# Packed output projections in four groups of 160 columns, and the fold's turn on VectorE

## The chip, the core and the metric

The kernel runs on one core of one Trainium2 chip. The metric is the device time of one execution in microseconds (us). Three executions of the kernel before took 4691.0, 4698.19 and 4706.44 us; the median is 4698.19 us. One further execution was taken with the hardware profiler; every row of a profile shown here is of that one.

A core has TensorE (PE in the rows; PEld are its weight loads), VectorE (DVE), ScalarE (ACT), GpSimd (POOL) and SyncE (SP). Each takes its own instructions in their written order and waits on semaphores for the others. SP only issues DMAs here; POOL issues DMAs too, and so, rarely, does ACT.

## The reference, cut to what matters

The program computes a forward pass and all gradients of two blocks that share a normalised input. Block B is a gated MLP over 2048 tokens of width 640. Block A, the one that matters here, is attention with a recurrent memory: the 2048 tokens are cut into T = 64 segments of 32, and each segment sees 8 memory rows that come from the output of the segment before.

```python
for s in range(n_seg):
    h = jnp.concatenate([mem, xs], axis=1)      # 8 memory rows and 32 tokens
    q, k, v = h @ Wq, h @ Wk, h @ Wv            # 32 heads of width 128
    p = softmax(where(mask, q @ k.T * scale, -1e9))
    o = einsum('bhte,hed->btd', p @ v, Wo)      # output projection: a sum over 32 heads of 128
    mem = o[:, :M, :]                           # 8 rows of 640 into the next segment
```

The memory makes block A serial: segment t+1 cannot begin before the 8 rows of segment t have been through the output projection. The gradient has the same chain backwards: the gradient of the 8 memory rows of segment t is a sum of three such projections, of the gradients of v, k and q with the weights turned, and segment t-1 needs it.

## The kernel before, in words

The work stands in phases: LayerNorm and the MLP forward; the forward recurrence (`recurrence`, L555); the backward recurrence (`phase4_Abwd`, L1083); the weight gradients; the MLP backward. Within the two recurrences the instruction order of every engine is the written order (`in_order`, L273, chains each engine's instructions). There is no scheduler that moves anything.

**A step.** Each recurrence calls `chain(t, gap)` once per segment, the forward one for t = 0 to 63, the backward one for t = 63 to 0. `chain` holds what depends on the memory rows, and at named places it calls `gap("W0")`, `gap("W1")`, ... `gap("G6")`. A gap puts work that does not depend on this step's memory in between: attention of the 32-token rows of the group of three segments before, in units of four heads (three units in most steps). In the forward recurrence such a unit goes through `scores`, `soft_max`/`soft_exp`, `norm` (a multiplication on POOL), `turn_p` (four transposes on PE and a copy on DVE, L835 to L841) and `pv`. In the backward one it goes through `ld` (four loads, all on SP's queue, L1289 to L1311), `turn`, `dprob`, `dsoft` (on DVE, L1350 and L1353) and `gmem`. A gap may end with `WARM` matmuls (L915, L1430), whose result nobody reads.

**The way round a forward step.** `hx` holds h transposed, 640 as five chunks of 128 partitions, with columns 0 to 7 for memory and 8 to 31 for tokens. `packed_half` (L301) multiplies it with Wk, Wq and Wv: the array of PE is used as four column groups of 32, each with its own 512 columns of weights as the moving operand. Then come the scores of the 8 memory rows, their softmax, P times v (L682), and `oTm` (L684, L685), the result transposed. `packed_out` (L317) is the output projection. Its rows are few, so it too uses four column groups: group 2a+b takes heads 16a to 16a+15 and output columns 320b to 320b+319. A call is 16 rounds of four matmuls with 320 moving columns, and every call leaves four partial results in the bank `pm`: two halves of the heads, times two halves of the columns.

The four parts are then folded and turned. `fold_add` (L330) lets ACT copy partitions 64 to 127 out of the bank (L334) and DVE add them to partitions 0 to 63 (L336, two halves), which gives `fsum` with 64 partitions: 32 rows for each half of the columns. `fold_turn` (L346) transposes the 8 memory rows with six small matmuls on PE against a selection matrix (L352). DVE copies the result into the next step's `hx` (L699), and the next step's Wk matmuls (L306) may start. `fsum` goes to the scratch tensor `FS` by one DMA from POOL (L700), and the gaps G5 and G6 stand around these pieces:

```python
packed_out(k, pm, oTm, Wo, True, True)
fs = fold_add(k, pm, ch)
gap("G5")
pt = fold_turn(k, bC, fs)
nc.vector.tensor_copy(nxt[:, :, 0:8], pt[:])
nc.gpsimd.dma_start(k.FS[t], fs[:])
gap("G6")
```

**The way round a backward step.** The same helpers are used. `packed_half` with WoT gives the gradient of o; the gradients of v (`gvT`), k (`gkT`) and q (`gqT`) of the memory rows follow; three `packed_out` calls with WvT, WkT and WqT accumulate into one bank (the first two cut in two pieces each, 5 + 11 and 4 + 12 rounds, around other work). Then `fold_add`, `gap("G4")`, `fold_turn`, `gap("G5")`, the copy into `gox` (the backward `hx`, L1283), and two DMAs from POOL into `GWO` (`fold_store`, L340 to L343), `gap("G6")`.

**Queues.** In a regular backward step SP issues, in this order: two stores of `dSm` (L1273), a load `xp` (L1174), the four loads of the unit freed in G3, the four of the unit freed in G5, the store of `GOS` (L1215), the four loads of the unit freed in W1, then the loads for the next step (L1151 to L1169). After the recurrences, a list `later` of DRAM-to-DRAM copies from `FS` is issued on POOL, one per backward step.

## Time and profile before

| what | value |
|---|---|
| median of three executions | 4698.19 us |
| the profiled execution | 4684.61 us |
| its span | 4682.7 us, granted clock 0.988 |
| forward recurrence, regular steps 3 to 62 | from 444.9 to 1563.8 us, a step is 18.7 to 19.2 us |
| backward recurrence, 64 steps | from 1821.5 to 2895.0 us, a step is 17.03 us |
| `packed_out` matmuls | 4032 forward, 12288 backward |
| `fold_turn` matmuls | 756 |

The steps were measured from the first matmul of one step's last `packed_out` to that of the next. A row of a view gives a start, a duration, the engine, the line, the operation and the tiles; in the grouped rows a duration is from the start of the first to the end of the last. A matmul's duration is a model, its start is recorded; so rates are read from starts.

### The profile page before, as it was taken

What the parts mean: (1) busy time and instruction counts of PE and PEld (TensorE: products, weight loads), DVE (VectorE), ACT (ScalarE), POOL (GpSimd) and SP (SyncE); (2) the same over time, 40 slices, a digit from 0 to 9 for tenths busy, and PEclk for the clock granted to TensorE, in tenths of its full rate; (3) what the DMA queues carried; (4) which work ended last, traced back from release to release, by engine and by line L of the source; (5) the groups of instructions that cost most, each with busy time, mean ns of one, the idle gap of its engine ahead of it and who ended that gap; (6) DMA issues with size and microseconds to landing.
All of it is one profiled execution on the core that took longest, in us unless ns stands there. A gap on an engine that the chain in (4) does not pass through costs nothing. (4 is left out here: it accounts for less than half of the span.)

```text
span 4682.7 us, 159785 instructions
## 1 busy us (share of the span) xinstructions
PE 4466.5 (95%) x64504; PEld 2821.1 (60%) x64504; DVE 2244.7 (48%) x7156; ACT 1587.4 (34%) x4360; POOL 2098.4 (45%) x3528
## 2 busy tenths in 40 slices
PE   8999999999999898999999998999999999999999
PEld 4544555555555555666666665676667666666675
DVE  8734666666666534555555553343224432311460
ACT  5432555555544433333333332232223322200000
POOL 6532555555555423455444444354335533311440
PEclk9999999999999998999999999999999999999999
DMA  8773566666655677777777775664345543579783
GB/s 269 236 252 119 175 178 178 179 179 179 180 168 167 167 181 230 211 225 207 215 211 209 208 209 154 144 163 132 110 116 158 147 129 107 170 223 207 159 181 100
DMA packets 976843, 834.77 MB, mean 178 GB/s; under 512 B 518890, under 2 KB 858286, under 8 KB 974144
## 3 DMA queue, kind: packets, MB, share of 16 engines
q1 hardware_dynamic: 763879, 547.92, 42.2%
q0 software_dynamic: 129952, 228.13, 16.4%
q10 hardware_dynamic: 82275, 48.52, 4.0%
q8 instruction: 509, 8.34, 0.8%
q14 instruction: 228, 1.87, 0.1%
HBM read 472.66 MB, written 310.33 MB: 167 GB/s over the span
## 5 line engine op out<-in xcount | busy, mean ns | idle before, releaser
L1667 PE MATMUL wg<-gr,hr 128*128 128x512 bf16 x2400 | 521.7, 379 | 0.0
L1648 PE MATMUL g<-land,ghacc 128*128 128x320 bf16 x3072 | 459.9, 300 | 0.8
L1667 PEld LDWEIGHTS <-hr 128*128 128x128 bf16 x2400 | 233.9, 98 | 278.9
L306 PEld LDWEIGHTS <-hx 128*32 128x32 bf16 x10240 | 246.8, 96 | 229.1 <-issue 14.6
L1648 PEld LDWEIGHTS <-ghacc 128*128 128x128 bf16 x3072 | 289.2, 98 | 104.2 <-ACT ghacc L92 2.2
L90 DVE CAST wgo<-wg 128x512 bf16<-128x512 f32 x72 | 49.8, 692 | 471.2 <-PE wg L1667 471.2
L90 DVE CAST stg<-bank 128x512 bf16<-128x512 f32 x256 | 177.1, 692 | 158.6 <-PE bank L306 154.5
L880 POOL DMA_DIRECT2D OR<-xv x163 | 89.8, 551 | 361.1 <-ACT xv L92 338.5
L1613 POOL DMA_DIRECT2D GSP<-grs x48 | 25.5, 542 | 473.1 <-ACT grs L1605 472.0
L92 ACT COPY ghacc<-t6g 128x768 bf16<-128x768 bf16 (+1 forms) x176 | 137.1, 779 | 293.8 <-PE t6g L1630 284.5
L1324 POOL DMA_DIRECT2D VTD<-gvT x176 | 129.4, 742 | 218.7 <-ACT gvT L1323 209.5
L325 PEld LDWEIGHTS <-gkv 128*8 128x8 bf16 x8192 | 177.6, 86 | 82.2 <-issue 4.1
L832 POOL TENSOR_TENSOR xP<-xP,xrz 120x480 bf16<-120x480 bf16 x163 | 161.1, 988 | 76.0 <-DVE xrz L831 46.6
L812 ACT ACTIVATE xP<-xsp,xnm 120x120 bf16<-120x120 f32 (+1 forms) x540 | 186.1, 372 | 26.0 <-DVE xnm L794 25.9
L1654 DVE TENSOR_TENSOR ghacc<-ghacc,g 128x320 f32<-128x320 f32 x192 | 93.6, 487 | 209.9 <-PE g L1648 209.9
L336 DVE TENSOR_TENSOR fsum<-bank,fup 64x160 bf16<-64x160 f32 x254 | 69.5, 311 | 258.5 <-ACT fup L334 255.2
L92 ACT CAST wgo<-wg 128x512 bf16<-128x512 f32 x48 | 28.1, 585 | 479.8 <-PE wg L1667 407.0
L1371 POOL DMA_DIRECT2D GXP<-gks x157 | 91.0, 580 | 189.5 <-ACT gks L1369 188.8
L325 PE MATMUL bank<-Wo,oTm 128*32 128x320 bf16 x4032 | 154.2, 307 | 18.4 <-DVE oTm L684 18.4
L325 PE MATMUL bank<-WkT,gkv 128*8 128x320 bf16 x4096 | 162.8, 299 | 4.2 <-issue 2.2
L325 PE MATMUL bank<-WvT,gkv 128*8 128x320 bf16 x4096 | 166.4, 305 | 0.5 <-DVE gkv L1197 0.5
L306 PE MATMUL bank<-Wq,hx 128*32 128x512 bf16 x2560 | 161.6, 381 | 0.0
(389 smaller groups left out, 10916.1 us busy)
## 6 DMA issues: line engine op xcount, KB each, us to landing
QVS<-stg SPq DMA_DIRECT2D x128, 256.0 KB
kT<-VTD SPq DMA_DIRECT2D x64, 320.0 KB
PR<-xP POOLq DMA_DIRECT2D x168, 120.0 KB, 3.1
VTD<-gvT POOLq DMA_DIRECT2D x168, 120.0 KB, 4.0
land<-DSR SPq DMA_DIRECT2D x168, 120.0 KB
land<-PR SPq DMA_DIRECT2D x168, 120.0 KB
OR<-xv POOLq DMA_DIRECT2D x163, 120.0 KB, 3.0
orr<-OR SPq DMA_DIRECT2D x14, 1280.0 KB
```

The lines of the kernel that those rows point to most:

```text
L90: return nc.vector.tensor_copy(out, in_)
L92: return nc.scalar.copy(out, in_)
L306: k.nc.tensor.matmul(bank[32 * g:32 * g + 32, :], x[:, dc, :], W[:, dc, c0:c0 + 512], start=(dc == 0), stop=(dc == k.DC - 1), tile_positio ...
L325: k.nc.tensor.matmul(pm[p0:p0 + nq, 0:320], x[:, h, :], W[:, h, 320 * b:320 * b + 320], start=(first and i == 0), stop=(last and i == 15), ...
L812: nc.scalar.activation(Pb[0:n, j, 0:n], sp[0:n, j, :], ACT.Exp, bias=nmx[0:n, j:j + 1], scale=k.scale, accum_out=Z[0:n, j:j + 1])
L832: eng.tensor_tensor(Pb[0:n, :, 0:n], Pb[0:n, :, 0:n], bc_last(rz[0:n], n), ALU.mult)
L880: q.dma_start(k.OR[120 * tl:120 * tl + n, c0:c0 + 512], v[0:n])
L1324: nc.gpsimd.dma_start(k.VTD[tl][:, :, h0:h0 + 4, :], vTq[:])
L1371: (nc.sync if (tl, qd) in pro else nc.gpsimd).dma_start(k.GXP[tl, :, qd, 0:ns], ks[:].rearrange("p s i h m -> p s i (h m)"))
L1648: nc.tensor.matmul(pg[:], ring[:, i, j, r0:r0 + P], Ws[qd][i][:, j, 320 * h:320 * h + 320], start=(i == 0 and j == 0), stop=(i == 2 and j ...
L1654: nc.vector.tensor_tensor(a, a, pg[:], ALU.add)
L1667: nc.tensor.matmul(pw[:], hr[:, tl, dc * P:(dc + 1) * P], grs[i][:, tl, :], start=(tl == 0), stop=(tl == NF - 1))
```

## The change

`packed_out` gives each column group 160 output columns over all 32 heads, in place of 320 columns over 16 heads. A call is now 32 rounds of four matmuls with 160 moving columns. Group g takes the columns whose index, in blocks of 32, is g modulo 4: its moving operand is five runs of 32 columns, 128 apart. No partial sums are left, so there is nothing to add. With this choice of columns a transpose of 32x32 blocks puts output column 128c + 32g + r of row m onto partition 32g + r, at place m of block c, which is where `hx` wants it.

`fold` takes the place of `fold_add` and `fold_turn`: one block transpose of the bank on DVE (128x160, fp32), a DVE copy of 8 of every 32 elements into the next `hx`, and then an ACT copy of the bank to bf16 for the store. `fold_store` now has four DMAs, one for each group, with runs of 32 elements (64 bytes), and it is issued on SP in both recurrences, where POOL had one (forward) or two (backward). In the built program these DMAs have the shape 160x1x32 forward and 40x1x32 backward; they stand on SP's queue after the unit loads of G5.

In the gaps: forward, `turn_p` of the second unit moves from G6 to W0 of the next step (after the Wk matmuls), `norm` of the third unit moves up into G5, G6 is gone, and G5's `WARM` goes from two matmuls to one. Backward, the gaps G4 and G5 follow each other after `fold`, and the one `WARM` matmul of G4 is gone. Pieces of the accumulation are cut at the same places (10 + 22 and 8 + 24 rounds). `FS` is now stored in the order of the output, so the `later` list has half as many copies.

```diff
-def packed_out(k, pm, x, W, first, last, i0=0, i1=16):
+def packed_out(k, pm, x, W, first, last, i0=0, i1=32):
 
     nq = x.shape[2]
-    for i in range(i0, i1):
-        for a in range(2):
-            for b in range(2):
-                h = 16 * a + i
-                p0 = 32 * (2 * a + b)
-                k.nc.tensor.matmul(pm[p0:p0 + nq, 0:320], x[:, h, :], W[:, h, 320 * b:320 * b + 320],
-                                   start=(first and i == 0), stop=(last and i == 15),
-                                   tile_position=(0, p0), skip_group_check=True)
+    for h in range(i0, i1):
+        w = W[:, h, :].rearrange("p (c g r) -> p g c r", g=4, r=32)
+        for g in range(4):
+            k.nc.tensor.matmul(pm[32 * g:32 * g + nq, 0:160].rearrange("p (c r) -> p c r", r=32), x[:, h, :], w[:, g],
+                               start=(first and h == 0), stop=(last and h == k.H - 1),
+                               tile_position=(0, 32 * g), skip_group_check=True)
 
-def fold_add(k, pm, pool, tag="fup"):
+def fold(k, pm, pool, dst, tag="fup"):
 
-    fs = pool.tile([64, 320], BF16, name="fsum", tag="fsum")
-    up = pool.tile([64, 320], F32, name="fup", tag=tag)
-    k.nc.scalar.copy(up[:], pm[64:128, 0:320])
-    for c in (0, 160):
-        k.nc.vector.tensor_tensor(fs[:, c:c + 160], pm[0:64, c:c + 160], up[:, c:c + 160], ALU.add)
+    if dst is not None:
+        tr = pool.tile([P, 160], F32, name="fup", tag=tag)
+        k.nc.vector.transpose(tr[:], pm[:, 0:160])
+        k.nc.vector.tensor_copy(dst, tr[:].rearrange("p (c m) -> p c m", m=32)[:, :, 0:8])
+    fs = pool.tile([P, 160], BF16, name="fsum", tag="fsum")
+    k.nc.scalar.copy(fs[:], pm[:, 0:160])
     return fs
 
 def fold_store(eng, dst, fs):
 
-    for b in range(2):
-        eng.dma_start(dst[:, 320 * b:320 * b + 320], fs[32 * b:32 * b + 8, :])
-
-
-def fold_turn(k, bank, fs):
...
+    n = dst.shape[0]
+    d = dst.rearrange("m (c g r) -> g m c r", g=4, r=32)
+    for g in range(4):
+        eng.dma_start(d[g], fs[32 * g:32 * g + n, :].rearrange("m (c r) -> m c r", r=32))
...
-        WARM = dict(G2=1, G3=2, G5=2)
+        WARM = dict(G2=1, G3=2, G5=1)
...
             packed_out(k, pm, oTm, Wo, True, True)
-            fs = fold_add(k, pm, ch)
+            fs = fold(k, pm, ch, hxs[(t + 1) % 2][:, :, 0:8])
             gap("G5")
-            pt = fold_turn(k, bC, fs)
-            nxt = hxs[(t + 1) % 2]
-            nc.vector.tensor_copy(nxt[:, :, 0:8], pt[:])
-            nc.gpsimd.dma_start(k.FS[t], fs[:])
-            gap("G6")
+            fold_store(nc.sync, k.FS[t], fs)
...
             if g == "W0":
                 oride_ld(t)
+                at(turn_p, t - 1, 1)
                 at(pv, t - 1, 0)
...
-            elif g == "G6":
-                at(turn_p, t, 1)
                 at(norm, t, 2)
...
-        WARM = dict(G4=1)
+        WARM = {}
...
             packed_out(k, pm, gqT, WqT, False, True)
-            fs = fold_add(k, pm, ch, "gstg")
+            fs = fold(k, pm, ch, goxs[(t - 1) % 2][:, :, 0:8] if t > 0 else None, "gstg")
             gap("G4")
-            if t > 0:
-                pt = fold_turn(k, bC, fs)
-                gap("G5")
-                nc.vector.tensor_copy(goxs[(t - 1) % 2][:, :, 0:8], pt[:])
-            fold_store(nc.gpsimd, k.m_rows(k.GWO, t - 1) if t > 0 else out2f, fs)
+            gap("G5")
+            fold_store(nc.sync, k.m_rows(k.GWO, t - 1) if t > 0 else out2f, fs)
             gap("G6")
```

More of the change, by code (lines that the diff above doesn't have):

```diff
@@ L172, in setup_dram @@
         self.OTX = mk("OTX", (self.NO, P, H, 24))
-        self.FS = mk("FS", (T, 64, 320))
+        self.FS = mk("FS", (T, 32, D))
         self.SR = mk("SR", (S, D))
@@ L346, in fold_turn @@
-def fold_turn(k, bank, fs):
-    pt = bview(bank, P, k.DC, 8)
-    for (dc, p0, c0, w, b) in ((0, 0, 0, 128, 0), (3, 0, 64, 128, 1), (2, 64, 0, 64, 1), (1, 0, 128, 128, 0),
-                               (4, 0, 192, 128, 1), (2, 0, 256, 64, 0)):
-        kw = {} if w == 128 else dict(tile_position=(0, p0))
-        k.nc.tensor.matmul(pt[p0:p0 + w, dc, :], fs[:, c0:c0 + w], k.sel[0:64, b, :], start=True, stop=True,
-                           skip_group_check=True, **kw)
-    return pt
+    n = dst.shape[0]
@@ L694, in chain @@
             packed_out(k, pm, oTm, Wo, True, True)
-            fs = fold_add(k, pm, ch)
+            fs = fold(k, pm, ch, hxs[(t + 1) % 2][:, :, 0:8])
             gap("G5")
-            pt = fold_turn(k, bC, fs)
-            nxt = hxs[(t + 1) % 2]
-            nc.vector.tensor_copy(nxt[:, :, 0:8], pt[:])
-            nc.gpsimd.dma_start(k.FS[t], fs[:])
-            gap("G6")
+            fold_store(nc.sync, k.FS[t], fs)
         WT = {}
@@ L1094, in phase4_Abwd @@
         tl0 = 1 if s == 0 else 0
-        for b in range(2):
-            dst = k.HRO[120 * tl0:120 * tl0 + 120 * (n - 1), :].rearrange("(t r) d -> t r d", r=120)[:, 96 + 8 * s:104 + 8 * s]
-            cols = slice(320 * b, 320 * b + 320)
-            later.append((dst[:, :, cols], k.FS[t0:t0 + 3 * (n - 1):3, 32 * b:32 * b + 8, :]))
-            t1 = t0 + 3 * (n - 1)
-            later.append((k.m_rows(k.HRO, t1 + 1)[:, cols], k.FS[t1, 32 * b:32 * b + 8, :]))
-    for b in range(2):
-        later.append((k.SR[0:24 * k.NO, 320 * b:320 * b + 320].rearrange("(t r) c -> t r c", r=24),
-                      k.FS[k.OT0:k.OT0 + k.NO, 32 * b + 8:32 * b + 32, :]))
+        dst = k.HRO[120 * tl0:120 * tl0 + 120 * (n - 1), :].rearrange("(t r) d -> t r d", r=120)[:, 96 + 8 * s:104 + 8 * s]
+        later.append((dst, k.FS[t0:t0 + 3 * (n - 1):3, 0:8, :]))
+        t1 = t0 + 3 * (n - 1)
+        later.append((k.m_rows(k.HRO, t1 + 1), k.FS[t1, 0:8, :]))
+    later.append((k.SR[0:24 * k.NO, :].rearrange("(t r) c -> t r c", r=24), k.FS[k.OT0:k.OT0 + k.NO, 8:32, :]))
     with tc.tile_pool(name="gst", bufs=1) as st, tc.tile_pool(name="gchain", bufs=1) as ch, \
@@ L1232, in chain @@
             gap("G1")
-            packed_out(k, pm, gvT, WvT, True, False, 0, 5)
+            packed_out(k, pm, gvT, WvT, True, False, 0, 10)
             ps2 = bview(bC, P, 2, 40, bf=True)
@@ L1247, in chain @@
                 loads(t - 1)
-            packed_out(k, pm, gvT, WvT, False, False, 5, 16)
+            packed_out(k, pm, gvT, WvT, False, False, 10, 32)
             gkT = gkv(0, Qst, bdS)
@@ L1255, in chain @@
             gap("G2")
-            packed_out(k, pm, gkT, WkT, False, False, 0, 4)
+            packed_out(k, pm, gkT, WkT, False, False, 0, 8)
             pgq = [bview(b_, P, 16, 8) for b_ in (bC, bB)]
@@ L1274, in chain @@
                                                           dS[:, a, c0:c1])
-            packed_out(k, pm, gkT, WkT, False, False, 4, 16)
+            packed_out(k, pm, gkT, WkT, False, False, 8, 32)
             gap("G3")
             packed_out(k, pm, gqT, WqT, False, True)
-            fs = fold_add(k, pm, ch, "gstg")
+            fs = fold(k, pm, ch, goxs[(t - 1) % 2][:, :, 0:8] if t > 0 else None, "gstg")
             gap("G4")
-            if t > 0:
-                pt = fold_turn(k, bC, fs)
-                gap("G5")
-                nc.vector.tensor_copy(goxs[(t - 1) % 2][:, :, 0:8], pt[:])
-            fold_store(nc.gpsimd, k.m_rows(k.GWO, t - 1) if t > 0 else out2f, fs)
+            gap("G5")
+            fold_store(nc.sync, k.m_rows(k.GWO, t - 1) if t > 0 else out2f, fs)
             gap("G6")
```

## The prediction

> **What bounds the kernel now.** The page's chain of waits covers only the last phase, so the recurrences are read from the trace by stage. Columns: window; its length; busy time and number of instructions of PE, weight loads, DVE, ACT, POOL; clock; DMA share; GB/s.

> ```profile
> 440.00:1560.00 1120.00, 1079.51 (x20885) 651.22 (x20882) 724.47 (x2032) 572.60 (x1866) 621.42 (x968) 1.00 0.59 176
> 1830.00:2840.00 1010.00, 967.90 (x22784) 638.06 (x22788) 541.97 (x2775) 339.20 (x1137) 493.25 (x895) 1.00 0.73 209
> ```

> PE is busy 96% of both, but a busy PE includes pipeline tails; the end of a step is set by the serial way round. The timeline of one forward step shows the piece that changes:

> ```profile
> 1001.04 2.36 PE L325 MATMUL bank<-Wo,oTm 128*32 128x320 bf16 x64 [0.29 <-DVE oTm L684]
> ...
> 1003.50 0.42 ACT L334 COPY fup<-bank 64x320 f32<-64x320 f32 x1 [0.68 <-PE bank L325]
> ...
> 1003.96 0.55 DVE L336 TENSOR_TENSOR fsum<-bank,fup 64x160 bf16<-64x160 f32 x2 [0.85 <-ACT fup L334]
> ...
> 1004.33 0.78 PE L352 MATMUL bank<-sel,fsum 64*128 64x8 bf16 x6
> ...
> 1005.04 0.38 PE L840 MATMUL xpp<-ident,xP 120*128 120x120 bf16 x4
> ...
> 1005.15 0.20 DVE L699 CAST hx<-bank 128x40 bf16<-128x40 f32 x1 [0.33 <-PE bank L352]
> 1005.40 2.34 PE L306 MATMUL bank<-Wk,hx 128*32 128x512 bf16 x40
> ```

> From the first packed matmul to the first Wk matmul: 4.36 us, every link waiting for the one before. All regular forward steps show 4.36. A backward step, the same links:

> ```profile
> 2386.19 2.35 PE L325 MATMUL bank<-WqT,gqT 128*8 128x320 bf16 x64
> ...
> 2388.59 0.42 ACT L334 COPY fup<-bank 64x320 f32<-64x320 f32 x1 [1.88 <-PE bank L325]
> ...
> 2389.04 0.55 DVE L336 TENSOR_TENSOR fsum<-bank,fup 64x160 bf16<-64x160 f32 x2 [2.86 <-ACT fup L334]
> 2389.41 0.78 PE L352 MATMUL bank<-sel,fsum 64*128 64x8 bf16 x6 [0.29 <-DVE fsum L336]
> ...
> 2390.23 0.20 DVE L1283 CAST hx<-bank 128x40 bf16<-128x40 f32 x1 [0.65 <-PE bank L352]
> ...
> 2390.58 2.34 PE L306 MATMUL bank<-WoT,hx 128*32 128x512 bf16 x40
> ```

> 4.39 us. Then SP's queue, which gets the four stores (line, operation, tiles, count: shortest/median/longest ns):

> ```profile
> L245 SPq DMA_DIRECT2D xq<-QVS x160: 269/617/1167, 422.0 to 1639.5; - x160
> L1156 SPq DMA_DIRECT2D kT<-QM x128: 577/627/1684, 1807.5 to 2871.5; - x128
> L1273 SPq DMA_DIRECT2D DSR<-dSm x128: 580/603/1742, 1820.1 to 2895.3; - x128
> ```

> Summing SP's timeline rows over 1838 to 2840 us gives per backward step 12.84 us issuing, 1.44 us in gaps under 0.15 us between instructions, and only 2.75 us in longer gaps, where it waits. In this excerpt it works without a rest:

> ```profile
> 2401.34 1.47 SPq L1167 DMA_DIRECT2D krb<-KS  x1
> 2402.91 1.26 SPq L1273 DMA_DIRECT2D DSR<-dSm  x2
> 2404.27 0.57 SPq L1174 DMA_DIRECT2D xp<-GXP  x1
> 2404.93 0.56 SPq L1307 DMA_DIRECT2D kT<-QVM  x1
> ```

> Forward it issues 9.9 and waits 7.5 us a step.

> [...] inside a four of `packed_out` the starts lie about 3 ns apart, and fours follow each other after 135 ns. [...] L682, in two row groups, starts one every 13 ns. [...] no transpose of DVE is in this trace. [...] moving the stores from POOL to SP moves issue time, here onto the fuller queue.

> **The change part by part.** *Packed matmuls.* Fours of 320 columns take 135 ns, fours of 512 (L306) 215 ns: 0.417 ns a column and 1.7 ns fixed. So 160 columns: 68.4 ns, and 32 fours take 2.19 us where 16 took 2.16. Two things could break this. Weight loads double in number: but after L325's first load the next three start 3 ns apart and their matmuls run 13 ns behind them, so the groups load side by side and 13 ns fits under 67. Issue must double to 8.5 ns an instruction: a semaphore instruction stands before L325 in 56 forward steps, and in the one at 1303 us 15 of the instructions after it were under way 80 ns after its end, 5.3 ns each.

> *Forward way round*, 0 at the first packed matmul. The last starts at 31 x 0.0684 + 0.03 = 2.15 us. The reader started 0.40 us after the last start; 160 columns fewer take 0.067 off: 2.48. The transpose: DVE rows on PSUM take 199 ns for 40 elements a partition, 311 for 160, 424 for 256; [...] I take 345 ns [...]. Then 30 ns, the copy 200 (as L699), 55 to the matmul: 3.11, saved 1.25. DVE's last instruction ends 0.4 us before it is wanted. PE's cover in G5 is 0.65 us, done at 2.84; the dropped `WARM` was cover alone. ACT's copy runs beside the transpose. `turn_p` leaves the shadow of the fold and lies in W0 between Wk and Wq, where PE has no wait: +0.21. POOL has done its input by then. Net -1.04 x 63 = -65 us. Four stores on SP (2.8 us, below) fit its 7.5 us; queued behind them are `oride`, wanted 8 us later, and the KS store, which has nearly 3 us before its buffer is rewritten and lands in 2.0 to 2.5.

> *Backward way round.* Last start 2.14; reader at + 0.352 - 0.067 = 2.42; + 0.345 + 0.03 + 0.20 + 0.146 = 3.14, saved 1.25; two further packed calls cost 0.03 each: net 1.19, a step of 15.84. PE's cover (the matmuls of G4 and G5, 0.5 us) ends at 2.7; DVE's `dsoft` follows `hx` as before.

> *SP backward.* The stores are 40x1x32. Rows of that form, n x 1 x m: L245 617 ns for 16 and 709 for 24, L1156 627 for 128; the store L1273, 16- and 64-byte runs, 603. Plain two-dimensional loads of few rows take 270 to 480. I take 650 and the usual gap of 46: 4 x 0.70 = 2.78, and SP needs 14.28 + 2.78 = 17.06 us a step. This is more than 15.84: the queue falls behind until unit loads come late (the last load of G3 is issued 5.4 us before its use) and TensorE waits for them. The step is 17.06 against 17.03: +2 us over 63. At 300 ns SP needs 15.66 and the chain decides: -75. At 1000 ns it needs 18.46: +90.

> *Elsewhere:* POOL loses 0.55 and 1.05 us a step, and was not waited for. The halved `later` list and the 64-byte runs in FS I put at nothing: 640 a step, at the mean 41 ns of a packet on SP's queue, are 1.6 us on each of 16 DMA engines, which are 59% busy.

> Sum: 4682.7 - 65 + 2 = 4620 for the span. The median shown is 13.6 us above the profiled 4684.6, so 4698 - 63 = 4635.

> **The rivals.** *B, both gain:* each store costs SP 450 ns or less. For: few rows, 8 partitions. Against: the n x 1 x m rows. -65, and -0.77 to -1.19 a step: 4558 to 4585. *C, the queue costs more than its sum:* stores of 850 ns or SP waits that stay, step 17.9 to 18.1 and the forward gain eaten: about 4695. *D, slower:* [...] a call takes 3.2 us, +1.03. Forward 0; backward 15.84 + 3 x 1.0 = 18.9, +1.87 x 63 = +118: 4816. It ends slower from 0.57 us a call, that is 21.4 ns a matmul. For: the fastest stretch of 320 TensorE instructions in this trace takes 15 ns each. Against: the 5.3 ns above. *That the change doesn't do what it says:* the built order shows the transposes and stores in place.

> **How the numbers follow.** My forecast A (forward gained, backward taken by SP) 0.48, B 0.22, C 0.18, D 0.12. A alone: 4600 to 4665. The range 4555 to 4725 takes in B, A and C, and leaves out D. About 0.3% (14 us) is what a measurement can tell from no change. Faster: A, B: 0.69; same: half of C: 0.09; slower: D and the other half: 0.22.

> **What would show it.** L325 groups of 128 matmuls spanning 2.3 to 2.4 us (D: 3.3); a DVE transpose near 345 ns; 3.1 us from first packed to first Wk or WoT matmul; forward steps near 17.7 us; SP's stores near 650 ns each and hardly a long gap left in SP's backward timeline, with TensorE waiting for loaded tiles at `turn`. Backward steps near 15.8 would make it wrong on SP, near 18.9 on the packed matmuls.

## The result, and the profile after

The changed kernel takes 4908.88 us in the median of four executions (4899.48 to 4916.46), the kernel before 4701.84 us beside it. The ratio is 1.0443, with a 95% interval of 1.0416 to 1.047: 207 us slower, where 63 us faster was predicted. The profiled execution took 4899.48 us, its span 4897.8 us. Of all executions behind this document two, one of the kernel before and one of the stores experiment, ran at a granted clock of 0.82 and 0.84 and took 5656 and 5244 us; no difference is read from them.

The forward recurrence lost little: a step takes 19.30 us on average against 18.98 before, times 61 steps 20 us. The backward one lost the rest: 20.35 us against 17.10, times 62 steps 201 us. From here on a step is counted from its first Wk (forward) or WoT (backward) matmul to that of the next; means are over 61 and 62 steps. Together that is 221 us; the two profiled spans differ by 215 us. First the two recurrences by window (window; length; busy time and number of instructions of PE, weight loads, DVE, ACT, POOL; clock; DMA share; GB/s):

```profile
440.00:1580.00 1140.00, 1008.61 (x24031) 646.71 (x24137) 738.37 (x1962) 554.99 (x1853) 583.49 (x904) 0.99 0.60 172
1850.00:3060.00 1210.00, 993.29 (x33819) 772.47 (x33820) 533.65 (x2721) 330.01 (x1142) 426.98 (x772) 0.96 0.62 176
```

Backward, PE now works through 67,639 instructions in 1210 us, 55.9 a microsecond, against 45,572 in 1010 us, 45.1, before. It is busy 82% of the time instead of 96%, and its clock is no longer 1.00. What PE waits for in that window (reason: us in total, times, longest us):

```profile
PE bank L323 <- issue: 139.8, 125, 2.4
PE bank L306 <- ACT fsum L335: 14.2, 46, 0.5
```

L323 is the packed matmul. "Issue" means that nothing in the profile held it: no semaphore, no other engine. The same row before, from 1830 to 2840 us:

```profile
PE bank L325 <- issue: 4.2, 5, 1.5
```

The timeline of one backward step shows where they lie, inside the runs of packed matmuls:

```profile
2101.18 1.48 PE L323 MATMUL bank<-WkT,gkv 128*8 128x160 bf16 x73
...
2104.72 0.59 PE L323 MATMUL bank<-WkT,gkv 128*8 128x160 bf16 x23 [2.05 <-issue]
2105.53 3.01 PE L323 MATMUL bank<-WqT,gqT 128*8 128x160 bf16 x97
2109.28 1.24 PE L323 MATMUL bank<-WqT,gqT 128*8 128x160 bf16 x31 [0.74 <-issue]
```

73 matmuls run at full pace, then PE stands for 2.05 us with 23 of the same call left. In the whole trace there are 146 such gaps of over 300 ns between neighbouring packed matmuls, 202.9 us in all; before there were 9, with 7.3 us. They are tied to a DMA queue that brings instructions. Its packets, MB and share of the 16 DMA engines, before and after:

```profile
q8 instruction: 509, 8.34, 0.8%
q8 instruction: 630, 10.32, 0.9%
```

Each packet is a block of 16 KB. TensorE has 130,486 recorded instructions before and 161,123 after, semaphore instructions included, about 256 for each block. In the gaps PE resumes 1.25 to 1.61 us after the end of the latest block's transfer (5th to 95th percentile), while a random moment of this stage lies 0.23 to 4.8 us after one.

A forward step, which should be compared with the one of before in the prediction:

```profile
993.52 2.40 PE L323 MATMUL bank<-Wo,oTm 128*32 128x160 bf16 x128 [0.37 <-DVE oTm L674]
...
995.96 0.35 DVE L332 STREAM_TRANSPOSE fup<-bank 128x160 f32<-128x160 f32 x1 [0.37 <-PE bank L323]
...
996.23 1.00 POOL L817 TENSOR_TENSOR xP<-xP,xrz 120x480 bf16<-120x480 bf16 x1
996.35 0.93 DVE L333 CAST hx<-fup 128x40 bf16<-128x40 f32 x1
...
997.34 0.61 PE L306 MATMUL bank<-Wk,hx 128*32 128x512 bf16 x8 [0.89 <-DVE hx L333]
```

This call is not interrupted, and the transpose takes 0.35 us as predicted. But the copy of 40 elements a partition takes 0.93 us instead of 0.2, and the way from the first packed to the first Wk matmul is 3.82 us, not 3.11. The four stores on SP's queue, minimum, median and maximum in ns:

```profile
L344 SPq DMA_DIRECT2D FS<-fsum x252: 554/601/1860, 390.8 to 1590.8; - x126
L344 SPq DMA_DIRECT2D GWO<-fsum x252: 646/694/1733, 1847.3 to 3104.5; - x126
```

The backward ones cost 694 ns where 650 was taken.

### The profile page after: what moved, and what is told of

It reads as the page before. It is cut to its first block, busy times and chain, and to the rows that moved or that the text cites. A ratio compares the mean times of both kernels' runs of the same rounds, so it can differ in the third digit from the quotient of the medians.

```text
span 4897.8 us, 190699 instructions
## 1 busy us (share of the span) xinstructions
PE 4400.5 (90%) x79723; PEld 2965.0 (61%) x79940; DVE 2250.2 (46%) x7028; ACT 1561.3 (32%) x4360; POOL 1989.3 (41%) x3330
## 4 chain that ended last, share of the span: by engine, by line
PE 53%; issue 5%; DMA 4%; DVE 2%; ACT 1%; SPq 0%; POOL 0%; ACTq 0%; POOLq 0%; DVEq 0%
PE wg L1644 11%; PE bank L323 10%; PE g L1625 8%; PE oa L1791 4%; PE bank L306 3%; PE wa L2179 2%; PE r6p L1575 2%; PE t6g L1607 2%; PE w2a L2035 1%; PE bank L1206 1%; PE pgxb L2112 1%; DMA land<-DSR 1%; DMA ggtok<-ggT 1%; DMA sl<-SLT 1%; PE bank L1242 1%
## 5 line engine op out<-in xcount | busy, mean ns | idle before, releaser
L306 PEld LDWEIGHTS <-hx 128*32 128x32 bf16 x10240 | 254.4, 98 | 310.8 <-issue 64.5
L323 PEld LDWEIGHTS <-gkv 128*8 128x8 bf16 x16384 | 287.1, 88 | 106.3 <-issue 88.6
L332 DVE STREAM_TRANSPOSE fup<-bank 128x160 f32<-128x160 f32 x126 | 44.1, 350 | 450.8 <-PE bank L323 450.8
L323 PE MATMUL bank<-WqT,gqT 128*8 128x160 bf16 x8192 | 184.7, 247 | 72.0 <-issue 71.8
L323 PE MATMUL bank<-WkT,gkv 128*8 128x160 bf16 x8192 | 187.3, 242 | 66.1 <-issue 64.3
L323 PEld LDWEIGHTS <-gqT 128*8 128x8 bf16 x8192 | 157.2, 92 | 86.9 <-issue 85.1
L323 PE MATMUL bank<-Wo,oTm 128*32 128x160 bf16 x8064 | 162.2, 239 | 42.7 <-issue 23.1
L306 PE MATMUL bank<-Wk,hx 128*32 128x512 bf16 x2560 | 155.5, 386 | 48.9 <-DVE hx L333 31.8
L306 PE MATMUL bank<-WoT,hx 128*32 128x512 bf16 x2560 | 169.0, 407 | 27.9 <-ACT fsum L335 17.3
L817 POOL TENSOR_TENSOR xP<-xP,xrz 120x480 bf16<-120x480 bf16 x163 | 161.4, 990 | 76.1 <-DVE xrz L816 47.2
```

The lines of the kernel that those rows point to most:

```text
L306: k.nc.tensor.matmul(bank[32 * g:32 * g + 32, :], x[:, dc, :], W[:, dc, c0:c0 + 512], start=(dc == 0), stop=(dc == k.DC - 1), tile_positio ...
L323: k.nc.tensor.matmul(pm[32 * g:32 * g + nq, 0:160].rearrange("p (c r) -> p c r", r=32), x[:, h, :], w[:, g], start=(first and h == 0), sto ...
L817: eng.tensor_tensor(Pb[0:n, :, 0:n], Pb[0:n, :, 0:n], bc_last(rz[0:n], n), ALU.mult)
```

## The experiments

Four explanations stood at the start. Theory 1: the doubled number of packed instructions outruns the supply of instructions. Rival 1: the stores on SP make loads late. Rival 2: the new fold itself is slow; one expectation calls its part on the slow copy theory 3. Rival 3: the removed `WARM` matmuls let the clock fall. Rival 4, added for the kernel that measures the supply by itself: data transfers delay the instruction blocks. Medians of the kernel before lie between 4693.48 and 4701.98 us in the comparisons.

### The doubled instructions alone

The kernel before, with each packed matmul in two halves, otherwise untouched:

```diff
-    for i in range(i0, i1):
-        for a in range(2):
-            for b in range(2):
-                h = 16 * a + i
-                p0 = 32 * (2 * a + b)
-                k.nc.tensor.matmul(pm[p0:p0 + nq, 0:320], x[:, h, :], W[:, h, 320 * b:320 * b + 320],
+    for i in range(i0, i1):
+        for c in (0, 160):
+            for g in range(4):
+                a, b = g // 2, g % 2
+                h, p0 = 16 * a + i, 32 * g
+                k.nc.tensor.matmul(pm[p0:p0 + nq, c:c + 160], x[:, h, :], W[:, h, 320 * b + c:320 * b + c + 160],
...
```

> The kernel before, with each packed matmul of 320 columns issued as two of 160, so that a packed call has 128 matmuls as after the change; fold, turn, stores and queues are those of before. Theory 1 (instruction supply): the doubled instructions alone starve TensorE inside the packed calls. In the changed kernel gaps over 250 ns between neighbouring packed matmuls sum to 204 us against 24 us before, and the half clock that follows comes on top; most of that should be here too, so 150 to 250 us over before: 4850 to 4950 us, with more than 100 such gaps that end 1.2 to 1.6 us after the end of an instruction fetch. Rival 1 (SP's queue with the four new stores) and rival 2 (the new fold, its copy and its waits): neither is in this kernel, so 4702 us plus 4 x 0.03 us x 63 = 4710 us, and no more gaps than before.

Measured: 5031.45 us, ratio 1.0697 (1.066 to 1.0735). The waits of PE from 1880 to 3250 us:

```profile
PE bank L325 <- issue: 152.9, 136, 3.0
```

This is above the 4850 to 4950 us that theory 1 expected, and far from the 4710 us of the rivals. The whole loss of the change, and more, comes without any part of its fold: 156 gaps over 300 ns, 214.2 us, PE resuming 1.25 to 1.59 us after the end of a block. That it is worse than the changed kernel fits its fold, which is the old one: 1.2 us longer a step, 126 times. These matmuls read 160 columns in one piece, the changed kernel's in five pieces of 32; so the pieces are not what slows them. Rivals 1 to 3 alone could not have done this.

### The instructions halved again, everything else kept

The changed kernel with 16 of the 32 heads, each over 320 columns: TensorE's work per call stays, the other heads are left out of the projections.

```diff
-    for h in range(i0, i1):
-        w = W[:, h, :].rearrange("p (c g r) -> p g c r", g=4, r=32)
+    for h in range(i0, i1, 2):
         for g in range(4):
-            k.nc.tensor.matmul(pm[32 * g:32 * g + nq, 0:160].rearrange("p (c r) -> p c r", r=32), x[:, h, :], w[:, g],
+            c0 = 320 * (g % 2)
+            k.nc.tensor.matmul(pm[32 * g:32 * g + nq, 0:320], x[:, h, :], W[:, h, c0:c0 + 320],
...
```

> The changed kernel with half of its packed matmuls: 16 heads of 32, each over 320 columns, so that a call has 64 matmuls and takes the same 2.16 us of TensorE; the other 16 heads and their share of the projection are left out. The new fold, the transposes and the four stores on SP stay. Theory 1: with the instructions back at the old number the gaps are gone and what the prediction said of the rest shows: forward gains 1.04 us a step less the slow copy (42 of 59 copies to hx took about 0.93 us instead of 0.18, 31 us in all), backward between SP's 17.06 us and the chain's 15.84 us a step: 4590 to 4680 us. Rivals 1 and 2: the time stays near 4909 us, since the stores and the fold are still there.

Measured: 4724.65 us, ratio 1.0054 (1.0035 to 1.0073). 184 of the 207 us are gone and so are the gaps, 2 left. But the time is above the range of theory 1: something else is left. Its waits of PE, 1850 to 2840 us:

```profile
PE gvpt L1297 <- DMA kT<-QVS: 33.8, 17, 4.0
PE gvpt L1297 <- DMA kT<-QVX: 21.5, 10, 4.0
```

This is `turn` waiting for loads of SP's queue, as the prediction described for a queue with too much to do. The backward step has a median of 15.97 us but a mean of 17.84: most steps run at the pace of the chain, SP falls behind, then a step stands for 1.2 to 4 us, and the clock is at half for 3.4 to 13.7 us after it (171 us of half clock in this recurrence). SP's rows, summed as in the prediction, are 16.97 us of work a step here (1850 to 2840 us), with 0.88 us of rest.

### The stores, twice

First on GpSimd again in the changed kernel, then in the kernel with half of the matmuls; the edit is the same:

```diff
-            fold_store(nc.sync, k.FS[t], fs)
+            fold_store(nc.gpsimd, k.FS[t], fs)
...
-            fold_store(nc.sync, k.m_rows(k.GWO, t - 1) if t > 0 else out2f, fs)
+            fold_store(nc.gpsimd, k.m_rows(k.GWO, t - 1) if t > 0 else out2f, fs)
```

> The changed kernel with its fold stores issued from GpSimd's queue, as before the change, instead of SyncE's. Theory 1: SP is not what delays the steps any more, because they have become longer than SP needs (17.06 us): 4909 us within 20 us. Rival 1: the stores on SP make unit loads late, and taking them away brings back most of 207 us: below 4760 us.

> The changed kernel with both edits of earlier runs: half of its packed matmuls (16 heads of 320 columns, the other heads left out) and the fold stores on GpSimd's queue. In the run with half of the matmuls alone the backward step had a median of 15.97 us but a mean of 17.80, and the long steps began with TensorE waiting 1.2 to 2.6 us at `turn` for a load of SyncE's queue, with half clock after it. Theory (SP's queue, the step of the prediction): without the stores these waits and the half clock behind them go, steps near 15.8 us on average, (17.80 - 15.8) x 63 = 126 us: 4590 to 4640 us. Rival (the long steps come from the fold's own idle time and the lower clock that it brings): 4725 us within 20 us, half clock still near 170 us in the backward recurrence.

Measured: 4914.75 us, the median of three executions (ratio 1.0454, 1.0418 to 1.0491), in the changed kernel: nothing that the interval could show. In the halved one 4625.82 us (ratio 0.985, 0.9835 to 0.9864), 99 us less. The waits of PE there, 1850 to 2780 us:

```profile
PE gvpt L1297 <- DMA kT<-QVS: 8.7, 7, 2.9
```

The median backward step is 15.88 us, the mean 16.57. So the stores on SP do cost about 100 us, but only once steps are shorter than what SP needs; in the changed kernel the starving PE makes steps of 20 us, and SP has time. A cause that is real can be invisible in an experiment that removes it alone.

### The slow copy, twice

The forward transpose writes into the free PSUM bank, and the copy reads it there:

```diff
-        tr = pool.tile([P, 160], F32, name="fup", tag=tag)
+        tr = bank[:, 0:160] if bank is not None else pool.tile([P, 160], F32, name="fup", tag=tag)[:]
...
-            fs = fold(k, pm, ch, hxs[(t + 1) % 2][:, :, 0:8])
+            fs = fold(k, pm, ch, hxs[(t + 1) % 2][:, :, 0:8], bank=bC)
```

> The changed kernel with one edit in the forward fold: the transpose writes into the third PSUM bank, which the removed turn used, and the copy to hx reads it from there instead of from SBUF. Theory 3 [...]: the forward copy took 0.93 us instead of 0.18 in 42 of 59 steps because it reads SBUF while GpSimd's multiply of the softmax (L817) runs, and a copy out of PSUM does not wait for it: every copy near 0.2 us, 31 us of copy time gone and most of it off the path, 4875 to 4895 us. Without that theory (the copy is slow for another reason, or lies off the path): 4909 us within 10 us, and slow copies still there.

> The kernel with half of the packed matmuls and the stores on GpSimd (4626 us; half of the heads left out), and the forward transpose written into PSUM, as in the earlier run that moved only that. Theory: with neither starved instructions nor SyncE's stores in the way, the slow copy of the forward fold is worth its time: 56 of 59 copies took 0.8 us too long, 46 us in all; the path from first packed to first Wk matmul falls from 3.82 to 3.2 us, and the time to 4580 to 4595 us. Without it (the copy lies beside other work that ends later): 4626 us within 8 us.

Measured: 4902.67 us (ratio 1.044, 1.0407 to 1.0472) in the changed kernel, 6 us less, which its interval does not tell from nothing. In the halved kernel with the stores on GpSimd: 4597.27 us (ratio 0.9781, 0.9766 to 0.9797), 29 us less. All 63 copies are near 0.2 us now, even the 39 in the changed kernel that lie wholly within a GpSimd instruction, as this row pair of the changed kernel with the edit shows:

```profile
1032.12 1.00 POOL L817 TENSOR_TENSOR xP<-xP,xrz 120x480 bf16<-120x480 bf16 x1
1032.24 0.20 DVE L333 CAST hx<-bank 128x40 bf16<-128x40 f32 x1
```

The forward path is 3.24 us there and 3.20 us in the halved kernel. In the changed kernel the forward step stayed where it was, 19.33 us against 19.30 without the edit; that the instruction supply took what the copy gave is likely, not shown.

### The removed WARM matmuls

```diff
-        WARM = dict(G2=1, G3=2, G5=1)
+        WARM = dict(G2=1, G3=2, G5=2)
...
-        WARM = {}
+        WARM = dict(G4=1)
```

> The changed kernel with the removed `WARM` matmuls put back (two in G5 forward, one in G4 backward). Rival 3 (the lower clock comes from their removal): the half clock, 119 us in the backward recurrence of the changed kernel and 15 us before, falls to some 30 us, and 50 to 100 us are gained: 4810 to 4860 us. Theory 1 (the clock drops because TensorE starves for instructions): one matmul of 0.2 us changes little, 4909 us within 20 us, half clock still above 90 us.

Measured: 4909.61 us, ratio 1.0446 (1.0424 to 1.0469), 106 us of half clock from the first to the last WoT matmul of the backward recurrence, against 119 without the edit. Rival 3 falls.

### The supply measured by itself

TensorE alone: packed calls one after the other, without a wait or a reader between them.

```python
for h in range(32):
    for g in range(4):
        nc.tensor.matmul(pm[32 * g:32 * g + 8, 0:160], x[:, h, 0:8], W[:, h % 8, 160 * g:160 * g + 160],
                         start=(h == 0), stop=(h == 31), tile_position=(0, 32 * g), skip_group_check=True)
```

> A kernel of its own that computes nothing of the reference: TensorE alone, packed calls one after the other without any wait, first 24 calls of 64 matmuls of 320 columns, then 12 calls each of 128 matmuls of 160, 200 and 240 columns, then calls of 160 columns with 4 to 40 matmuls of 512 columns between them, and last 12 calls of 160 columns while SyncE streams weights in. Theory 1: instructions arrive in blocks of 256, and in all traces so far two fetches never start less than 3.3 us apart. If that is the limit, a call of 128 matmuls (256 instructions) takes 3.3 to 3.7 us whether its columns are 160 (2.19 us of work), 200 (2.7) or 240 (3.27), a call of 64 matmuls of 320 columns (128 instructions) takes its 2.16 us, and calls of 160 columns run at full speed once about 1.2 us of other work lies between them, that is from 8 matmuls of 512 columns on. It is the same with and without data traffic. Rival 4 (the fetches are slow because data transfers delay them): 2.19, 2.7 and 3.27 us a call without traffic, longer only in the last part. Rival (packed matmuls limited by issue): a fixed time per matmul, no gaps of a microsecond tied to fetches.

Measured in one execution, first a stretch of 320 columns, then the beginning of the calls of 160 columns with DMA idle, then two calls while SyncE streams weights (DMA share 1.01, 419 GB/s):

```profile
23.82 10.36 PE L17 MATMUL pm<-W,x 128*8 128x320 bf16 x300
```

```profile
82.89 4.53 PE L38 MATMUL pm<-W,x 128*8 128x160 bf16 x251
88.00 2.39 PE L38 MATMUL pm<-W,x 128*8 128x160 bf16 x128 [0.58 <-issue]
91.45 2.39 PE L38 MATMUL pm<-W,x 128*8 128x160 bf16 x128 [1.07 <-issue]
```

```profile
500.88 2.39 PE L45 MATMUL pm<-W,x 128*8 128x160 bf16 x128 [2.46 <-issue]
507.37 4.44 PE L45 MATMUL pm<-W,x 128*8 128x160 bf16 x128 [4.10 <-issue]
```

At 320 columns none of the 1536 matmuls comes more than 126 ns after the one before it, and the 24 calls take 2.17 us each. At 160 columns the first 251 matmuls, with their loads some 500 instructions, run at full pace, 8.6 ns an instruction; from there on 128 matmuls come, then a gap, then 128 again: exactly one block of 256 instructions each time. Twelve calls take 41.64 us at 160 columns, 41.74 at 200 and 42.03 at 240, almost the same whatever the work in them. These sums contain the first calls, which ran at full pace. After them the blocks start 3.65 us apart on average at 160 columns (3.43 to 4.06) and 3.60 at 200: some 14 ns an instruction. At 240 columns, where a call is 3.27 us of work, the first gap comes only after 643 matmuls. With 4 matmuls of 512 columns between the calls short gaps of 0.24 to 0.39 us remain; with 8 (1.7 us of work) there is none. Under full DMA load the twelve calls take 69.5 us, part of it at half clock (granted clock 0.80 over this stretch), and the blocks start 6.17 us apart (5.93 to 6.68). So theory 1 holds, and rival 4 is half right: the limit is there without traffic, and traffic raises it by about two thirds.

The times of the blocks show what the distance is made of: a transfer takes 1.0 us, the first of its instructions runs 1.4 us after its end, and the next block's transfer starts 1.1 us after that in most rounds, up to 1.7 in the others. Under load the last term is 3.5 to 4.1 us while the transfer is still 1.0; what fills it the profile does not show.

So PE can use up packed matmuls of 160 columns faster than they come: 8.6 ns an instruction in the first 251 with their loads, against some 14 ns from block to block with DMA idle and 24 ns under load (6.17 us for 256).

### How much doubling is too much

Only the last of the three backward calls doubled, in the kernel before:

```diff
-            packed_out(k, pm, gqT, WqT, False, True)
+            packed_twice(k, pm, gqT, WqT, False, True)
```

> The kernel before with only the last of the three backward packed calls (WqT) doubled to 128 matmuls of 160 columns: 3.5 blocks of 256 instructions a step instead of 3.0. If the average supply decides (blocks about 4.6 us apart in this stage, 3.5 x 4.6 = 16.1 us, less than the step of 17.03 us): 4702 us within 15 us. If each doubled call starves by itself, because at most two blocks are held and a call uses one in 2.2 us: 0.8 to 1.4 us of waiting in most steps, 50 to 90 us more: 4750 to 4790 us. In both cases far less than the 336 us of doubling all four calls.

Measured: 4734.22 us, ratio 1.0083 (1.0058 to 1.0109): +32 us, between the two expectations, a tenth of what doubling all four calls costs (+336). The doubled call takes 2.60 us from first to last start in the mean against 2.10 before (2.29 against 2.05 in the median), and its row of waits names issue only 17 times in that stage (16.8 us). So neither the average nor the single burst decides alone. A quarter of the doubled calls costs a tenth of the time: the loss grows faster than the count.

### Looking for a version that gains

The runs say: keep the number of matmuls and the stores on POOL, and shorten the fold. Three attempts move the sum of the two head halves into the turn on PE, whose matmuls then contract over all 128 partitions. (Beside the lines shown, their edits add the selection `sel2` and put two small constants into one tile.) In the first, ScalarE and VectorE cast half of the columns each:

```diff
-    k.nc.scalar.copy(up[:], pm[64:128, 0:320])
-    for c in (0, 160):
-        k.nc.vector.tensor_tensor(fs[:, c:c + 160], pm[0:64, c:c + 160], up[:, c:c + 160], ALU.add)
+    k.nc.scalar.copy(fc[:, 0:160], pm[:, 0:160])
+    k.nc.vector.tensor_copy(fc[:, 160:320], pm[:, 160:320])
...
-        k.nc.tensor.matmul(pt[p0:p0 + w, dc, :], fs[:, c0:c0 + w], k.sel[0:64, b, :], start=True, stop=True,
+        k.nc.tensor.matmul(pt[p0:p0 + w, dc, :], fs[:, c0:c0 + w], k.sel2[:, b, :], start=True, stop=True,
```

> A version built on what the runs show: the 64 matmuls of 320 columns a call, the turn on TensorE, `WARM` and the stores on GpSimd stay as before the change; only the sum of the two head halves moves into the turn. ScalarE and VectorE each cast 160 columns of all 128 partitions to bf16 at the same time (0.29 and 0.31 us instead of 0.42 + 0.05 + 0.55 us one after the other), and the six matmuls of the turn add the halves by contracting over 128 partitions; the rows to be stored are summed afterwards by two matmuls and a copy, off the path. If the fold is on the path as the prediction read it, a step saves some 0.6 to 0.7 us in both recurrences: 4702 - 126 x 0.65 = 4620 us (4600 to 4650). If shortening the fold is not worth its time on the path: 4700 us.

Measured: 4716.86 us, ratio 1.0046 (1.0037 to 1.0055): slower. The timeline of a backward step tells why:

```profile
2392.27 0.29 ACT L336 CAST fup<-bank 128x160 bf16<-128x160 f32 x1 [1.88 <-PE bank L328]
...
2392.59 0.33 DVE L337 CAST fup<-bank 128x160 bf16<-128x160 f32 x1 [2.35 <-ACT fup L336]
```

VectorE's cast waits on a semaphore for ScalarE's, which reads the same PSUM bank and writes the same tile, and two matmuls that sum the rows for the store stood in front of WoT (0.36 us). In the second attempt ScalarE casts alone and the row sums come after half of the next step's first product (the diff is against the first attempt):

```diff
-    k.nc.scalar.copy(fc[:, 0:160], pm[:, 0:160])
-    k.nc.vector.tensor_copy(fc[:, 160:320], pm[:, 160:320])
+    k.nc.scalar.copy(fc[:], pm[:, 0:320])
...
             packed_half(k, bA, gox, WoT, 0)
+            if t + 1 in owed:
+                fold_store(nc.gpsimd, k.m_rows(k.GWO, t), fold_rows(k, bC, ch, owed.pop(t + 1)))
```

> A second attempt at a shorter fold that keeps the 64 matmuls of 320 columns: in the first one VectorE's cast waited for ScalarE's, which reads the same PSUM bank (0.65 us one after the other), and the two matmuls that sum the rows stood before the next step's first matmul (0.36 us), so the path from the first packed to the first WoT matmul stayed at 4.32 us against 4.39. Here ScalarE alone casts all 320 columns (0.42 us), the turn follows at once, and the row sums come after the first half of the next step's Wk or WoT matmuls. Expected path 4.39 - 0.05 - 0.35 to 0.55 = 3.8 to 4.0 us, 0.4 to 0.6 us a step, 50 to 75 us: 4630 to 4655 us. If the backward step of 17.03 us is set by something other than the path through the fold, only forward gains: 4670 us.

Measured: 4722.11 us, ratio 1.0051 (1.0033 to 1.0069). Slower again. The backward path through the fold fell from 4.39 to 3.92 us, and the two sum matmuls put the same 0.5 us between the halves of WoT (last WoT start 2.47 us after the first instead of 1.96). The third takes the row sums off PE (against the kernel before, the added lines alone):

```diff
+    k.nc.scalar.copy(fc[:, 0:320], pm[:, 0:320])
+    k.nc.scalar.copy(fc[0:64, 320:640], fc[64:128, 0:320])
...
+    k.nc.vector.tensor_tensor(fs[:], fc[0:64, 0:320], fc[0:64, 320:640], ALU.add)
```

> The shorter fold once more, with the row sums taken off TensorE: in the run before, the path from first packed to first WoT matmul fell from 4.39 to 3.91 us, but the two sum matmuls of 320 columns put 0.5 us between the halves of the WoT matmuls. Here ScalarE casts all 320 columns (0.42 us), TensorE turns and sums, and the rows are summed in SBUF: a second copy of ScalarE moves the upper 64 partitions down beside the turn, and VectorE adds after its copy to hx, where it has more than 1 us before the first Wk or WoT half is ready. Instructions of TensorE as before the change. Expected: 0.4 to 0.5 us a step off the path in both recurrences, 126 x 0.45 = 57 us: 4635 to 4660 us. If the backward step is held at 17 us by SyncE's queue (14.3 us of work a step) or another engine, only forward gains: 4670 us.

Measured: 4651.99 us, ratio 0.9911 (0.9898 to 0.9925): 41 us faster than the kernel before, which took 4693.48 us beside it. Its backward step:

```profile
2383.99 2.35 PE L328 MATMUL bank<-WqT,gqT 128*8 128x320 bf16 x64
...
2386.39 0.43 ACT L336 CAST fup<-bank 128x320 bf16<-128x320 f32 x1 [1.88 <-PE bank L328]
...
2386.87 0.59 PE L360 MATMUL bank<-sel,fup 128*128 128x8 bf16 x6 [0.15 <-ACT fup L336]
...
2387.91 2.34 PE L309 MATMUL bank<-WoT,hx 128*32 128x512 bf16 x40 [0.16 <-DVE hx L1292]
```

3.92 us from the first packed to the first WoT matmul, and nothing added elsewhere; the backward step has a median of 16.55 us, against 17.03 before. This version beats both kernels.

## Why the prediction was wrong, point by point

**Packed matmuls: the step that failed.** The prediction said: "Issue must double to 8.5 ns an instruction", and let it pass because "15 of the instructions after it were under way 80 ns after its end, 5.3 ns each". The 5.3 ns are right for 15 instructions, and the first 500 in a row do run at 8.6 ns. A call has 256, and in the backward step three calls come close together. The supply of some 14 ns an instruction with DMA idle, and 24 ns under load, was never asked for; a row that hinted at it, "the fastest stretch of 320 TensorE instructions in this trace takes 15 ns each", was put under a rival with a chance of 0.12. In place of "32 fours take 2.19 us": in undisturbed calls yes (2.164 us from first to last start), but the three calls of a backward step last 10.9 us together in the median, against 7.0 in the halved kernel with the stores on GpSimd. These 3.9 us are most of what the two median steps (20.23 and 15.88 us) differ by.

**Rival D**, issue that bounds the packed matmuls at 25 ns each (the distance at which the 32 score matmuls of L647 start in the trace of before), named the right place, and 118 of the 207 us: 3.2 us a call, 4816 us. The cause is another one, since an undisturbed call runs at 2.164 us, and forward, which D put at 0, was not free of it.

**SP backward** was right, hidden in the changed kernel and visible in the halved one: predicted 17.06 us a step, mean 17.84, of which SP works 16.97; stores 694 instead of 650 ns. What the sum left out is that the queue still rests (0.88 us a step) and that half clock follows the stalls (171 us in the halved kernel's backward recurrence); how much each costs is not separated. Rival C had this size (17.9 to 18.1).

**The chain** was right: 3.14 us from first packed to first WoT matmul was predicted and 3.13 measured (halved kernel), a step of 15.84 against a median of 15.88; the transpose 345 against 350 ns (345 was the author's estimate; the trace of before has no such transpose, and its DVE rows of 160 elements out of PSUM took 311 ns). "ACT's copy runs beside the transpose" was not: it waits on a semaphore for the transpose, which reads the same bank, and in the backward recurrence starts 33 ns after its end. WoT then starts 51 ns after ACT's copy and, in the median, 0.160 us after the copy into `gox`, where the sum had 0.146 us: this mistake was nearly free by luck. Forward it shows once the copy into `hx` is fast: in the halved kernel with that copy in PSUM, Wk starts 51 ns after ACT's copy and 0.198 us after the copy into `hx`, where the sum had 0.055 us.

**Forward**: "the copy 200 (as L699)" took the wrong row. L699 reads PSUM; the new copy reads SBUF, and 42 of 59 took about 0.93 us, 31.5 us in all. Every slow copy lies beside L817, a GpSimd multiplication of about 1 us, and ends 48 to 54 ns after it; out of PSUM the copy took about 0.2 us all 63 times. What holds the copy from SBUF back the profile does not show. With the copy out of PSUM the forward step gains 0.94 us (18.04 against 18.98) where 1.04 was predicted.

**Sum.** Taking the causes out one after the other: 4908.88, without the doubled instructions 4724.65, without SP's stores 4625.82, without the slow copy 4597.27 us. The last three leave out half of the heads. The order matters: the last two removed alone changed nothing that can be told from zero. The second figure also says that with a free supply the forecast of 4635 us would still have been some 90 us too low, for the queue and the slow copy; that 4724.65 us lies within the stated range is luck.

**What stays open**: what the half clock costs by itself was not separated from the waits that it follows, and the lists and FS rows that were put at nothing were not tried.

## What to carry to other kernels

Count a change's instructions, not only its work: where matmuls get shorter and more, compare the time that 256 of their instructions take with the 3.65 us measured here, over stretches longer than two blocks, and with more under DMA load (6.17 us with DMA full, a median of 4.3 us after the gaps of the changed kernel's backward recurrence, at a DMA share of 0.62). When two limits are stacked, removing the lower one alone may show nothing, as here; test it again after the upper one is gone. When a result is moved from PSUM to SBUF, look at what GpSimd does while it is read: here the copy took about 0.93 us from SBUF beside L817, 0.18 us in all 63 backward steps, and 0.2 us from PSUM.
